# Pooled attention and a top-1 MoE on one core: V summed on two engines in the opening, another order of the first two units, K and V turned in full shapes, two weight pieces on GpSimd

## Chip, cores and metric

One core of a Trainium2 chip runs the whole program as one launch. The metric is device time in microseconds (us), median of three runs. Engines: PE (TensorE: matmuls and transposes), DVE (VectorE), ACT (ScalarE), POOL (GpSimd), SP (SyncE, which issues most transfers).

## The reference

```python
# q, k, v: (8 batches, 8 heads, 576 rows, 64), float32
k_p = k.reshape(B, H, 72, 8, D).mean(axis=3)        # 576 rows of K pooled to 72
v_p = v.reshape(B, H, 72, 8, D).mean(axis=3)
attn = softmax(scale * q @ k_p.T)                   # (.., 576, 72); 1e-9 is added to the sum
x = (attn @ v_p), heads side by side                # (4608 tokens, 512)
logits = x @ w_gate                                 # 8 experts
e, gate = argmax(logits), softmax(logits)[argmax]   # one expert for each token
y = gate * (relu(x @ w1[e]) @ w2[e])                # 512 -> 1024 -> 512
```

## The kernel before

**Attention** takes the span to about 182 us, **MoE** the rest. A *unit* is 128 query rows with all 8 heads: four units for each batch, and one more for the leftover rows of each pair of batches, 36 in all. Units go in groups of two. For a group `g_qt` (L477) turns q on PE, and ACT copies it to `qT`. `g_s` (L500) computes scores into one of two `ps` buffers, `g_min` (L510) takes the row maxima on DVE, `g_exp` (L517) is four exponentials on ACT. For a unit `u_pt` (L524, L526) turns P on PE and copies it on ACT, `u_pv` (L546) multiplies P by V into `po`, of which there is one buffer, and `u_nrm` (L573 to L575, DVE) divides by the row sums and so frees `po`. V is held in `VB` as [V | V times gate weights | 1], so `u_pv` yields the router's logits too.

**K and V of a batch** are loaded by SP into three buffers `kv[3]` (K of batch b in `kv[2b%3]`, V in `kv[(2b+1)%3]`). Their 576 rows lie in five chunks of 128 partitions, the last half full. The sum of 8 rows is made for b >= 2 on POOL in three steps (`pool`: L338 on 128x1280, L340 on 128x640, L341 on 128x320). `k_pe` turns K on PE (L379) into 64 partitions of PSUM, `k_act` copies that into half 0 of the block-diagonal `BD` (L391), and a transfer in ACT's queue (`moves`, L1037) copies half 0 to half 1. `v_pe` (L403, L405, and L407 for K's last 64 rows) turns V, `u_pe` (L424) multiplies it by the gate weights, and three operations on DVE lay the result into `VB`: `gates` (L431, reads PSUM), `masked_low` and `masked_high` (L436, two SBUF inputs: the sum of V and the mask `mk`).

**Order.** The code before L800 writes out the opening (batch 0: DVE sums K by `pool_now` and V by `pool_sum`, L360; the first scores; K of batch 1 summed on POOL from L812 and on DVE). Then one loop over the 36 units writes the code of each in a fixed order; `put(unit, position, f, args)` hangs more work at positions in it ("q" ahead of the unit, "pe", "act", "dve", "dve3", "sp"). Routing operations and the three that lay V are `fillers`, taken from a list a few at a time behind `u_pv`. `on_beat` makes a POOL operation wait for the last instruction in the list `beat`, which is the reciprocal (L574) of the unit before. `idle(n)` writes matmuls without use on PE, wide (512 columns) or narrow (128). `lsplit` (L868) makes the low part of the first expert's weights on DVE, in four pieces for each of eight j, pieces j=0 and 1 in units 13 to 16 and 18 to 21.

**MoE** is a loop over blocks of 256 tokens of one expert. Its tail takes the two halves of the finished block and scatters their rows: `give(1)`, then `give(0)` (L1278 on POOL), whatever the number of tokens.

## Time and profile before

| quantity | value |
|---|---|
| three runs | 595.24, 592.2, 591.74 us; median 592.2 |
| profiled execution, its own time | 594.74 us (span of the profile 592.1) |
| PE busy | 567.0 us, 96% of the span |
| DVE, ACT, POOL busy | 306.5, 276.4, 241.4 us |
| read from and written to memory | 73.65 and 23.37 MB |

The span is the time from the first to the last instruction of the profiled execution; the difference to its own time is what lies around it. PE is busy nearly everywhere, so what counts is PE's work itself, the places where PE stands idle, and the clock that it is granted (PEclk, 1.00 is 2.4 GHz). A row of stretches gives, for each engine, busy us and (x) the number of instructions. A row of the timeline is: start us, us, engine, line, operation, out<-in, xcount, and in brackets the idle time ahead of it and what ended it.

### The profile page before, as it was taken

Reading aid. Unit: us, or ns where it says so; the run is one execution under the profiler, and the core shown is the slowest. Engines: PE = TensorE matmul, PEld = TensorE weight load, DVE = VectorE, ACT = ScalarE, POOL = GpSimd, SP = SyncE. Lnnn points to the kernel's source line nnn. Section 1 sums busy time; section 2 is a strip of 40 time slices with the busy share of each in tenths; the row PEclk is TensorE's granted clock in tenths of the full one; section 3 lists DMA queues with packets and bytes.
Section 4 is the critical chain, followed back from the end, with each engine's and each line's share of the span. In section 5 each row is a group of like instructions: output and inputs, shape, how many; then the busy total and the mean of one; then the engine's idle time right before and its main releaser. Section 6 shows DMA issues by size and latency. Waiting matters only on the chain. (4 is left out here: it accounts for less than half of the span.)

```text
span 592.1 us, 15018 instructions
## 1 busy us (share of the span) xinstructions
PE 567.0 (96%) x4332; PEld 423.3 (71%) x4333; DVE 306.5 (52%) x639; ACT 276.4 (47%) x627; POOL 241.4 (41%) x465
## 2 busy tenths in 40 slices
PE   7989999999999989999999999999999999999993
PEld 6778998889885755775676676765767657767571
DVE  5776779997798272128312221272313723182783
ACT  4666788878942362227222222261223622272771
POOL 6495889884545222122222012231122311224255
PEclk8998999999999999999999999999999999999998
DMA  9997999857357959952943214339143491319310
GB/s 278 299 313 196 327 336 344 255 173 277 98 187 230 287 154 360 347 123 65 335 134 91 53 58 111 90 66 351 58 111 84 95 352 38 105 35 333 75 45 12
DMA packets 94072, 107.76 MB, mean 182 GB/s; under 512 B 53894, under 2 KB 62086, under 8 KB 94040
## 3 DMA queue, kind: packets, MB, share of 16 engines
q1 hardware_dynamic: 86408, 85.46, 49.6%
q0 software_dynamic: 6640, 20.99, 9.5%
q10 hardware_dynamic: 992, 0.92, 0.6%
q8 instruction: 16, 0.26, 0.2%
q14 instruction: 16, 0.13, 0.1%
HBM read 73.65 MB, written 23.37 MB: 164 GB/s over the span
## 5 line engine op out<-in xcount | busy, mean ns | idle before, releaser
L1067 PEld LDWEIGHTS <-bd 128*128 128x128 f16 x936 | 91.2, 98 | 105.7 <-DVE bd L1061 0.8
L1061 DVE SCALAR_TENSOR_TENSOR bd<-ps,bd 128x512 f16<-128x512 f32 (+1 forms) x44 | 27.5, 630 | 143.7 <-ACT bd L1057 143.2
L1277 POOL TENSOR_TENSOR spacer<-ql,iG 1x1 f32<-1x1 f32 x44 | 18.5, 420 | 166.2 <-ACT ql L1273 154.1
L517 ACT ACTIVATE both<-ps,nmx 128x72 f32<-128x72 f32 x288 | 70.0, 350 | 12.6 <-DVE nmx L510 12.2
L1067 PE MATMUL po<-w,bd 128*128 128x512 f16 x264 | 59.1, 379 | 0.0
L1067 PE MATMUL po<-kv,bd 128*128 128x512 f16 x264 | 58.8, 379 | 0.0
L546 PE MATMUL po<-vb,pt 128*128 128x146 f32 (+1 forms) x320 | 52.7, 311 | 5.5 <-DVE both L575 4.6
L1278 POOL DMA_INDIRECT out_dram<-ql,iG x44 | 47.1, 1071 | 22.0 <-issue 20.6
L1057 ACT ACTIVATE bd<-ps 128x512 f16<-128x512 f32 (+1 forms) x44 | 23.8, 547 | 69.2 <-PE L987 56.4
L546 PEld LDWEIGHTS po<-vb,pt 128*128 128x128 f32 x320 | 46.5, 192 | 8.4 <-issue 5.2
L1067 PE MATMUL pq<-kv,bd 128*128 128x512 f16 x216 | 48.1, 379 | 0.0
L989 PE MATMUL ps<-kv,qt 128*128 128x256 f16 (+1 forms) x176 | 44.8, 263 | 0.9 <-DVE qt L115 0.9
L677 POOL DMA_INDIRECT x_by_expert<-both,rpos x36 | 35.8, 996 | 23.2 <-issue 6.2
L987 PE MATMUL ps<-kv,w 128*128 128x256 f16 (+1 forms) x176 | 43.1, 258 | 2.3 <-DVE bd L906 1.8
L500 PE MATMUL ps<-bd,qT 128*128 128x144 f32 x256 | 45.0, 301 | 0.0
L987 PE MATMUL ps<-kv,qt 128*128 128x256 f16 (+1 forms) x176 | 44.8, 263 | 0.0
L988 PE MATMUL ps<-kv,qt 128*128 128x256 f16 (+1 forms) x176 | 44.8, 263 | 0.0
L989 PE MATMUL ps<-kv,w 128*128 128x256 f16 (+1 forms) x176 | 43.1, 258 | 0.0
L988 PE MATMUL ps<-kv,w 128*128 128x256 f16 (+1 forms) x176 | 43.1, 258 | 0.0
L1067 PE MATMUL pq<-w,bd 128*128 128x512 f16 x192 | 42.7, 379 | 0.0
L338 POOL TENSOR_TENSOR st<-kv 128x1280 f32<-128x1280 f32 x13 | 37.7, 2901 | 12.0 <-DVE ri L574 7.0
L1273 ACT ACTIVATE ql<-po,gB 128x512 f32<-128x512 f32 x22 | 15.1, 685 | 55.5 <-PE L987 41.6
(246 smaller groups left out, 1274.4 us busy)
## 6 DMA issues: line engine op xcount, KB each, us to landing
st<-in_moe_w_dram SPq DMA_DIRECT2D x8, 2048.0 KB, 13.8
both<-in_moe_w_dram SPq DMA_DIRECT2D x6, 2048.0 KB, 12.9
vb<-x_by_expert SPq DMA_DIRECT2D x16, 578.0 KB
kv<-in_v_dram SPq DMA_DIRECT2D x16, 512.0 KB
kv<-in_k_dram SPq DMA_DIRECT2D x7, 1024.0 KB
qt<-in_q_dram SPq DMA_DIRECT2D x7, 1024.0 KB
st<-in_moe_w_dram SPq DMA_DIRECT2D x4, 1024.0 KB
kv<-in_v_dram SPq DMA_DIRECT2D x8, 208.0 KB
```

The source lines that it names most:

```text
L338: on_beat(nc.gpsimd.tensor_tensor(t1, src[:, :, 0:4 * D], src[:, :, 4 * D:], op=OP.add))
L500: nc.tensor.matmul(ps[:, x * 2 * KP:(x + 1) * 2 * KP], t[:, h, :], BD[b % 3][:, :, h, :], start=True, stop=True)
L517: nc.scalar.activation(p[:, h * KP:(h + 1) * KP], ps[:, x * KP:(x + 1) * KP], AF.Exp, bias=nmx[:, x:x + 1], scale=-1.0)
L546: nc.tensor.matmul(po[:, cols], a[:, c * 128:(c + 1) * 128], VB[b % 3][:, c, sl, 0:CW], start=h in (0, LEFT), stop=False, skip_group_check ...
L677: st = nc.gpsimd.indirect_dma_start(out=xs, out_offset=bass.IndirectOffsetOnAxis(ap=Z["pos"][:, u:u + 1], axis=0), in_=X[:, u, :], in_offs ...
L987: nc.tensor.matmul(dst, wh, xT[:, d, 0:n], start=(d == 0), stop=False)
L988: nc.tensor.matmul(dst, wh, xT[:, DC + d, 0:n], start=False, stop=False)
L989: nc.tensor.matmul(dst, wl, xT[:, d, 0:n], start=False, stop=(d == DC - 1))
L1057: nc.scalar.activation(h, p, AF.Relu)
L1061: V.scalar_tensor_tensor(l, p, 0.0, h, op0=OP.max, op1=OP.subtract)
L1067: nc.tensor.matmul(y, hT[x][:, f, 128 * j:128 * j + 128], W2[s][z][:, f, :], start=(half == x == z == f == 0), stop=(half == z == 1 and f ...
L1278: st = nc.gpsimd.indirect_dma_start(out=out, out_offset=bass.IndirectOffsetOnAxis(ap=iG[:, j:j + 1], axis=0), in_=ys[j], in_offset=None, b ...
```

## The change

- **Opening.** V of batch 0: DVE sums three chunks, POOL two (`pool_pool`). V's chunks are laid in another order (`VK`, `HS`, `SLOTS`: the short one first). The warming matmuls go from 54 ahead of everything to 46 there, 22 narrow ones behind the turn of the gate weights and 4 more; that turn stands ahead of the second half of K, with three copies on ACT for five. The idle matmuls go from 5 wide to 11 wide.
- **Units 0 and 1** are written out by hand (`if i == 0`, `if i == 1`); `u_pt(1)` comes ahead of the turn of K of batch 1. That K is laid out doubled (`k1`, with three copies by `same` on DVE), so that it is turned by four full transposes and one small one, where it was four transposes, four matmuls and two small ones.
- **K and V of later batches** stand in one tile of ten 64-wide columns (`kvp`) and are turned as pairs, 128 columns at once: two transposes for K and three for V. K leaves PSUM in two copies, and its transfer becomes two.
- **Laying V:** `masked_low`, `masked_high`, `gates`, in that order; for batch 1 the two enter `beat`. The first step of V's sum of batch 2 on POOL moves to position "dve3" of unit 3.
- **Weights:** j=0 and 1 (eight operations of DVE) become `gsplit`, four 128x1024 operations of POOL in units 24, 25, 27 and 28.
- **Tail of the MoE loop:** `give(1)`, `give(0)` only where the block has more than one half filled, else the other way round.

```diff
-WARM = 54
+WARM = (46, 22, 4)
-VK = (0, 128, 216, 344, 472)
+VK = (472, 0, 128, 216, 344)
...
     def k_pe(b):
-        for c in range(4):
-            nc.tensor.transpose(pm[0:64, c * 128:(c + 1) * 128], kp[:, c], ident)
...
+        if b > 1:
+            for x in range(2):
+                nc.tensor.transpose(pm[:, 128 * x:128 * x + 128], pair(kp, 2 * x), ident)
+        else:
+            for x, o in enumerate((0, 1, 3, 4)):
+                nc.tensor.transpose(pm[:, 128 * x:128 * x + 128], pair(k1, o), ident)
...
     def k_act(b):
...
+            for s in range(2):
+                nc.scalar.activation(other(b, s, s), pm[64 * s:64 * s + 64, 0:256].rearrange("p (a x) -> p a x", a=2),
+                                     AF.Copy, scale=-SC)
+                moves.append((other(b, 1 - s, s), other(b, s, s), b))
...
     def v_pe(b):
...
+        for x in range(3):
+            nc.tensor.transpose(pm[:, x * 128:x * 128 + 128], pair(kvp, 4 + 2 * x), ident)
...
+            if b == 1:
+                beat.append(done)
...
-        fillers[0:0] = [(-1, False, f) for f in (gates, masked_low, masked_high)]
+        fillers[0:0] = [(-1, False, f) for f in (masked_low, masked_high, gates)]
...
+    def pool_pool(src, dst, c, out=None):
+        nc.gpsimd.tensor_tensor(t1[:, c], src[:, c, 0:4 * D], src[:, c, 4 * D:], op=OP.add)
+        nc.gpsimd.tensor_tensor(t2[:, c], t1[:, c, 0:2 * D], t1[:, c, 2 * D:], op=OP.add)
+        for o, i in out or ((c, c),):
+            nc.gpsimd.tensor_tensor(dst[:, o], t2[:, i, 0:D], t2[:, i, D:], op=OP.add)
...
-    pool_sum(kv[1], vp, slice(0, 1))
+    pool_sum(kv[1], vp, slice(1, 2))
+    pool_pool(kv[1], vp, slice(3, 5))
+    idle(5)
...
-    for c in range(2, 5):
-        pool_sum(kv[1], vp, slice(c, c + 1))
+    pool_sum(kv[1], vp, slice(2, 3))
+    pool_sum(kv[1], vp, slice(0, 1))
...
-                        put(POOLAT[b] + x + y, "q", f, b, y)
+                        put(*((3, "dve3") if (b, x, y) == (2, 2, 0) else (POOLAT[b] + x + y + (b == 2 and x == 2), "q")),
+                            f, b, y)
...
+    def gsplit(j, part):
+        src, t = st1[0][:, j], scratch[j]
+        if part == 0:
+            on_beat(nc.gpsimd.tensor_tensor(t, src, swc[:, 0:1].to_broadcast([128, F]), op=OP.mult))
+        else:
+            on_beat(nc.gpsimd.tensor_tensor(W1[0][1][:, j], t, W1[0][0][:, j], op=OP.subtract))
+
+    for at, j, x in ((24, 0, 0), (25, 0, 1), (27, 1, 0), (28, 1, 1)):
+        put(at, "q", gsplit, j, x)
...
+        if i == 0:
+            run(i, "q")
+            u_pv(0)
+            g_s(*A)
+            g_exp(*Y)
+            g_min(*A)
+            g_exp(*A)
+            u_pt(1)
+            run(i, "sp")
+            g_s(*Z)
+            u_nrm(i, lambda: g_min(*Z))
+            pool_k1(1)
...
+            g_qt(*turns[0])
+            continue
...
-        give(1)
...
-        give(0)
+        either(many > 1, lambda: [give(j) for j in (1, 0)], lambda: [give(j) for j in (0, 1)])
```

The next two pieces are DVE's instructions around the laying of V of batch 1 (`vb_161` before, `vb_162` after), ahead of unit 4's norm; the first is of before, the second of the change.

```order
L575 TENSOR_TENSOR both<-po,ri 128x576
L510 TENSOR_REDUCE nmx<-ps 128x4 x2
L431 TENSOR_TENSOR vb_161<-pq,mk 128x15x8
L436 TENSOR_TENSOR vb_161<-vp,mk 128x3x2x64
L436 TENSOR_TENSOR vb_161<-vp,mk 128x6x64
L573 TENSOR_SCALAR ri<-po 128x8
```

```order
L585 TENSOR_TENSOR both<-po,ri 128x576
L520 TENSOR_REDUCE nmx<-ps 128x4 x2
L444 TENSOR_TENSOR vb_162<-kvp,mk 128x3x2x64
L444 TENSOR_TENSOR vb_162<-kvp,mk 128x2x3x64
L438 TENSOR_TENSOR vb_162<-pq,mk 128x15x8
L583 TENSOR_SCALAR ri<-po 128x8
```

The two operations with two SBUF inputs (L436, now L444) have moved ahead of the one that waits for PE (L431, now L438); nothing else is between the two norms.

Next PE around the turn of K of batch 1 (L379 to L386 before, L391 and L393 after): `bd_157` and `bd_158` are the block-diagonal K of batches 0 and 1 before, `bd_159` that of batch 1 after; L524 and L534 turn P of unit 1.

```order
L500 MATMUL ps<-bd_157,qT 128x144 x2
L477 MATMUL pq<-ident,qt_154 128x128 x4
L379 MATMUL pq<-ident,kp 64x128 x4
L382 MATMUL pq<-ident,kp 64x128 x4
L385 MATMUL pq<-ident,kp 64x64
L386 MATMUL pq<-ident,kp 64x64
L500 MATMUL ps<-bd_157,qT 128x144 x2
L524 MATMUL pp<-ident,both 128x128 x5
L500 MATMUL ps<-bd_158,qT 128x144 x2
```

```order
L534 MATMUL pp<-ident,both 128x128 x5
L510 MATMUL ps<-bd_158,qT 128x144 x2
L487 MATMUL pq<-ident,qt_155 128x128 x4
L556 MATMUL po<-vb_161,pt 128x146 x3
L556 MATMUL po<-vb_161,pt 128x219
L556 MATMUL po<-vb_161,pt 128x146
L391 MATMUL pq<-ident,st_64 128x128 x4
L393 MATMUL pq<-ident,st_64 128x64
L487 MATMUL pq<-ident,qt_155 128x128 x4
L510 MATMUL ps<-bd_159,qT 128x144 x4
```

The turn of P of unit 1 (L534) and its P·V (L556) have moved ahead of the turn of K, which is half as many instructions; behind it only one turn of q stands ahead of the first scores that need it.

Last POOL in units 24 to 28, where the pieces of the first weights have come in between the scatters of tokens (L687): L911 multiplies, L913 subtracts.

```order
L911 TENSOR_TENSOR kv_152<-st_64,swc 128x1024
L686 MEMSET spacer 1x1
L687 DMA x_by_expert<-both,rpos 38016x578
L913 TENSOR_TENSOR w_01_61<-kv_152,w_00_60 128x1024
L686 MEMSET spacer 1x1
L687 DMA x_by_expert<-both,rpos 38016x578
```

Between them stood only the scatters before; the pair comes a second time for the other piece.

## Rows read from the trace of the kernel before

**Rows 1.** Stretches: window, length, busy us of PE, PEld, DVE, ACT, POOL; clock; DMA.

```profile
10.30:17.80 7.50, 7.50 (x36) 6.55 (x37) 4.65 (x8) 5.01 (x21) 0.00 (x0) 0.54 1.08 303
17.80:42.10 24.30, 22.98 (x173) 20.60 (x171) 17.36 (x29) 17.90 (x59) 18.32 (x11) 1.00 1.08 300
42.10:44.60 2.50, 0.02 (x1) 0.00 (x1) 2.43 (x5) 0.00 (x0) 2.42 (x3) 1.00 1.04 354
44.60:48.40 3.80, 3.77 (x16) 3.74 (x17) 2.12 (x7) 2.29 (x9) 2.68 (x2) 0.55 1.07 261
48.40:88.00 39.60, 38.42 (x320) 35.36 (x320) 27.87 (x81) 30.05 (x106) 30.96 (x28) 1.00 0.94 287
88.00:126.00 38.00, 35.31 (x301) 33.22 (x298) 35.43 (x93) 29.86 (x101) 33.08 (x31) 1.00 0.90 286
126.00:182.00 56.00, 55.33 (x486) 50.28 (x484) 46.30 (x169) 40.63 (x127) 30.96 (x55) 1.00 0.54 185
182.00:592.00 410.00, 397.39 (x2952) 268.05 (x2950) 164.02 (x228) 147.86 (x203) 114.00 (x296) 0.99 0.50 149
```

**Rows 2.** Timeline of the opening: the sum of V, the first P·V.

```profile
17.26 2.93 DVE L360 TENSOR_REDUCE vp<-kv 128x64 f32<-128x512 f32 x3
18.28 1.82 POOL L812 TENSOR_TENSOR st<-kv 128x768 f32<-128x768 f32 x1 [8.09 <-DMA kv<-in_k_dram]
...
20.11 1.89 DVE L436 TENSOR_TENSOR vb<-vp,mk 128x256 f32<-128x256 f32 x3
...
23.16 1.53 PE L546 MATMUL po<-vb,pt 128*128 128x146 f32 x10
...
27.39 2.90 POOL L338 TENSOR_TENSOR st<-kv 128x1280 f32<-128x1280 f32 x1 [4.94 <-DMA kv<-in_v_dram]
...
27.53 1.20 ACT L391 ACTIVATE bd<-pq 64x512 f32<-64x512 f32 x2 [0.35 <-PE pq L382]
```

**Rows 3.** Timeline at 38 us: POOL's sum beside DVE's laying of V.

```profile
38.25 2.90 POOL L338 TENSOR_TENSOR st<-kv 128x1280 f32<-128x1280 f32 x1
...
38.39 3.18 DVE L436 TENSOR_TENSOR vb<-vp,mk 128x384 f32<-128x384 f32 x1
...
38.39 4.99 DVE L436 TENSOR_TENSOR vb<-vp,mk 128x384 f32<-128x384 f32 x2
...
41.22 1.74 POOL L340 TENSOR_TENSOR st<-st 128x640 f32<-128x640 f32 x1
...
44.63 0.67 PE L546 MATMUL po<-vb,pt 128*128 128x146 f32 x2 [2.51 <-DVE both L575]
```

**Rows 4.** Timeline of PE's weight loads: a batch's V turn, then its K turn.

```profile
49.90 0.25 PEld L403 LDWEIGHTS pq<-ident,vp 128*128 128x128 f32 x2
50.12 0.11 PEld L405 LDWEIGHTS pq<-ident,vp 128*64 128x64 f32 x1
50.42 0.11 PEld L407 LDWEIGHTS pq<-ident,kp 64*64 64x64 f32 x1 [0.20 <-issue]
50.60 0.55 PEld L546 LDWEIGHTS po<-vb,pt 128*128 128x128 f32 x4
...
39.43 0.45 PEld L379 LDWEIGHTS pq<-ident,kp 128*64 128x64 f32 x4
39.88 0.55 PEld L500 LDWEIGHTS ps<-bd,qT 128*128 128x128 f32 x4
```

**Rows 5.** Stretches of the weight pieces L868 alone: length, DVE busy (count).

```profile
86.00:123.00 37.00, 6.82 (x8) 1.00 0.94 297
123.00:182.00 59.00, 10.61 (x24) 1.00 0.54 184
```

**Rows 6.** Transfers in ACT's queue (L1037): ns min/median/max, first and last start.

```profile
L1037 ACTq DMA_DIRECT2D bd<-bd x12: 468/468/553, 46.1 to 139.9; - x12
```

**Rows 7.** Timeline of POOL at the end: the last two scatters.

```profile
584.58 1.00 POOL L1278 DMA_INDIRECT out_dram<-ql,iG  x1 [0.56 <-issue]
...
586.62 1.00 POOL L1278 DMA_INDIRECT out_dram<-ql,iG  x1 [0.56 <-issue]
```

More of the change, by code (lines that the diff above doesn't have):

```diff
@@ L370, in pool_v, with pair, other @@
-        pool(kv[(2 * b + 1) % 3], KVS["vp", b], (part,))
+        pool(kv[(2 * b + 1) % 3], KVS["kvp", b][:, 5:10], (part,))
+    def pair(x, o):
+        return x[:, o:o + 2, :].rearrange("p c d -> p (c d)")
     def half(b, s):
         return BD[b % 3][64 * s:64 * s + 64, s].rearrange("p h x -> p (h x)")
+    def other(b, s, c):
+        return half(b, s)[:, 0:512].rearrange("p (a c x) -> p a c x", a=2, c=2)[:, :, c]
     def k_pe(b):
-        kp = KVS["kp", b]
+        kp = KVS["kvp", b]
         pm = KVS["pk", b] = psA.tile([128, 512], F32, name="pq", bufs=2)
-        for c in range(4):
-            nc.tensor.transpose(pm[0:64, c * 128:(c + 1) * 128], kp[:, c], ident)
@@ L380, in k_pe @@
-        if b == 1:
-            for c in range(4):
-                nc.tensor.matmul(pm[64:128, c * 128:(c + 1) * 128], kp[:, c], ident, start=True, stop=True)
-            pm, kt, it = psA.tile([128, 512], F32, name="pq", bufs=2), kp[0:64, 4], ident[0:64, 0:64]
-            KVS["pt", b] = pm
-            nc.tensor.transpose(pm[0:64, 0:64], kt, it)
-            nc.tensor.matmul(pm[64:128, 0:64], kt, it, start=True, stop=True)
+        if b > 1:
[4 more added lines that the diff above has]
+                nc.tensor.transpose(pm[:, 128 * x:128 * x + 128], pair(k1, o), ident)
+            pt = KVS["pt", b] = psA.tile([128, 512], F32, name="pq", bufs=2)
+            nc.tensor.transpose(pt[:, 0:64], pair(k1[0:64], 6), ident[0:64, 0:64])
@@ L399, in v_pe @@
+        nc.scalar.activation(half(b, 0)[:, 0:512], pm[0:64, :], AF.Copy, scale=-SC)
+        for c in range(2):
+            nc.scalar.activation(other(b, 1, 1 - c), pm[64:128, :].rearrange("p (a c x) -> p a c x", a=2, c=2)[:, :, c],
+                                 AF.Copy, scale=-SC)
+        pm = KVS.pop(("pt", b))
+        for s in range(2):
+            nc.scalar.activation(half(b, s)[:, 512:576], pm[64 * s:64 * s + 64, 0:64], AF.Copy, scale=-SC)
     def v_pe(b):
-        vp, kp = KVS["vp", b], KVS.pop(("kp", b), None)
+        kvp = KVS["kvp", b]
@@ L535, in u_pv @@
         PO_[i] = po[:, o0:o0 + H * CW]
-        for c in range(5):
+        for c in (1, 2, 3, 4, 0):
             sl = slice(*SLOTS[c])
@@ L733, in idle @@
                 nc.tensor.matmul(warm[:, 0, 0:128], ones, ones, start=True, stop=True)
-    vp = KVS["vp", 0] = work.tile([128, 5, D], F32, name="vp", bufs=2)
+    KVS["kvp", 0] = pooled(0)
+    nc.gpsimd.memset(KVS["kvp", 0][:, 4], 0.0)
+    vp = KVS["kvp", 0][:, 5:10]
     kp = st1[1].rearrange("p c x -> p (c x)")[:, 160:800].rearrange("p (c a d) -> p c a d", c=5, a=2)
-    KVS["kp", 1] = work.tile([128, 5, D], F32, name="kp", bufs=2)
-    idle(WARM, False)
+    KVS["kvp", 1] = pooled(1)
+    nc.gpsimd.memset(KVS["kvp", 1][:, 4], 0.0)
+    idle(WARM[0], False)
     constants()
@@ L767 @@
     k_keep(1, 0, 256)
+    turn_gates()
+    idle(WARM[1], False)
     pool_now(kv[0], kp, Z)
+    load_kv(1, vf)
     g_qt(0, 0)
+    idle(WARM[2], False)
     k_first((2, 3, 4))
-    k_keep(1, 256, 576)
     g_s(0, 0)
     k_keep(0, 256, 576)
+    k_keep(1, 256, 576)
     g_min(0, 0)
@@ L784 @@
     g_exp(0, 2)
-    pool_sum(kv[1], vp, slice(1, 2))
-    idle(2)
     g_s(0, 3)
@@ L789 @@
     g_exp(0, 3)
-    for c in range(2, 5):
-        pool_sum(kv[1], vp, slice(c, c + 1))
+    pool_sum(kv[1], vp, slice(2, 3))
+    pool_sum(kv[1], vp, slice(0, 1))
     gates, masked = u_dve(0)
+    load_kv(2, kf)
+    load_ql(0)
     g_qt(1, 0)
-    idle(2)
+    idle(4)
     u_pt(0)
+    g_s(1, 0)
     v_pe(0)
@@ L834, in prep @@
         put(u[0], "dve", u_dve, b)
-    prep(1, (0, "2"), (2, "2"), (3, ""))
+    put(2, "pe2", v_pe, 1)
+    put(2, "act2", v_act, 1)
+    put(3, "pe", u_pe, 1)
+    put(3, "dve", u_dve, 1)
     put(1, "sp", load_kv, 3, kf)
@@ L1002 @@
         Y = halves.get(2 * i - 1)
+        if i == 0:
[10 more added lines that the diff above has]
+            pool_k1(1)
+            same(k1[:, 2], k1[:, 0])
+            same(k1[:, 5], k1[:, 3])
+            same(k1[0:64, 7], k1[0:64, 6])
+            load_kv(2, vf)
+            g_qt(*turns[0])
+            continue
+        if i == 1:
+            run(i, "q")
+            g_exp(*Y)
+            u_pv(1)
+            u_nrm(i)
+            k_pe(1)
+            k_act(1)
+            g_qt(*turns[1])
+            run(i, "sp")
+            g_s(*A)
+            g_min(*A)
+            g_exp(*A)
+            g_s(*Z)
+            g_min(*Z)
+            continue
         if i < 30 and aged:
```

103 lines of the change are left out of this document (46 added, 57 removed).

## The prediction, made before the changed kernel had run

> **What bounds the kernel now.** I read first the page's busy shares, then the table of stretches, then the timeline where that table shows PE idle. PE is busy 567.0 of 592.1 us, so a gain must come from PE's own work, from its idle time, or from stretches at the lower clock. The stretches sort this [rows 1]. The MoE stretch (182 to 592) is 397 of 410 us PE at clock 0.99: the change touches only its tail. In the attention PE is idle 1.3 us in 17.8–42.1, 2.5 us in one piece at 42.1–44.6, 1.2 in 48.4–88, 2.7 in 88–126 and 0.7 in 126–182. The granted clock is 0.54 in 10.3–17.8 and 0.55 in 44.6–48.4, near the lower of the two levels; the second of these begins directly behind the idle 2.5 us.
>
> In the opening the first P·V starts at 23.16, at the end of a DVE chain: three V sums of 0.98 us from 17.26, then the laying of V from 20.11 [rows 2]. At 38 us there is another chain. POOL's first step of V's sum for batch 2 starts at 38.25 and takes 2.90. DVE's laying of batch 1 (two SBUF inputs) starts at 38.39 and shows 3.18 us, ending at 41.57, hardly after POOL has ended at 41.15. The second laying of the pair (together 4.99) runs beside POOL's next step, 41.22 to 42.96 [rows 3]. The norm that frees `po` queues behind both on DVE, and the P·V that waits for it comes at 44.63, after 2.51 us that ended with DVE's L575 [rows 3].
>
> The same collision is seen more weakly on the weight pieces: 8 pieces cost DVE 6.82 us at 86–123, where POOL sums batches, and 24 pieces 10.61 us at 123–182, 0.85 against 0.44 each [rows 5].
>
> **The change part by part.**
>
> *A, opening.* Two V sums leave DVE: 2 x 0.98 = 2.0 us earlier for the first P·V, if POOL has its two chunks ready in time; five chunks took 2.90 for the first step [rows 2], so two are far cheaper. Of this I take back 0.9: PE now reaches batch 1's turn of K with only one turn of q ahead of the scores that need it (the second pair of fences), and ACT's two copies of that K took 1.20 [rows 2]; they are now three. The copies were hidden by two turns and older scores before. The fillers and the earlier turn of the gate weights may keep the clock up in 10.3–17.8; at full clock that stretch's work would be 7.50 x 0.46 = 3.4 us shorter. I count none of it, since DVE's chain and not PE sets 23.16, but it is the upper bound's reason. On the other side DVE's laying of batch 0 could block with POOL's sum of K, which is about 1.82 in its first step [rows 2]. A: **+1.1**, bounds -1 to +2.2.
>
> *B, the stall at 42.* Now the two layings stand ahead of `gates`, thus do not wait for PE, and POOL's first step of batch 2 is ordered behind them by `beat` (first pair of fences). Alone they cost about the 1.89 that three such took in the opening [rows 2]. What goes: 2.5 us idle, and the low clock behind it, 3.8 x 0.45 = 1.7 [rows 1]. POOL's sum of V of batch 2 gets some 2 to 4 us later; it is needed only when batch 2 is turned, near 49.9 [rows 4]. Its first two steps ended at 42.96 [rows 3] and the third is half as large as the second, so over 5 us were to spare and the lateness hides. B: **+4.2**, bounds 2 (idle time returns in part, in smaller pieces that leave the clock alone) to 4.2.
>
> *C, turns in full shapes.* A batch's V turn spans 49.90 to 50.60, 0.70 with the gap of 0.20 ahead of the 64x64 one, and its K turn 39.43 to 39.88, 0.45 [rows 4]: 1.15. Now it is five instructions of 0.125: 0.62. Gain 0.53 for each of six batches (b=2 to 7), 3.2, and an estimated 0.1 each for `u_pe`, which waits for one copy of V instead of two: 3.8 in all. PE is 97–99% busy in 48.4–88 and 126–182 [rows 1], so most of it counts; in 88–126 DVE ends the waits and PE's work is hidden. I take about two thirds: **+2.6**, bounds 0 to 3.8.
>
> *D, eight weight pieces off DVE.* They take 6.82 us of DVE in 86–123 [rows 5], where DVE is busy 35.4 of 38 and PE is idle 2.7 [rows 1]. At most the 2.7 goes. Part of it is POOL against the routing operations, which stays. **+1.2**, bounds 0 to 2.7.
>
> *E, four GpSimd operations and six more transfers.* A 128x1024 operation lies between 1.82 (768) and 2.90 (1280): about 2.35 us [rows 2]. POOL has room, 31.0 busy of 56 in 126–182 [rows 1]. DVE's remaining pieces (j=2 and 3, units 22–25 and 27–30) meet them; by rows 5 a piece that meets POOL's work is 0.4 us longer, some eight pieces, 3.3 us on a DVE that has 10 of 56 free: **-0.5**, bounds 0 to -2.5. The K transfers in ACT's queue go from 12 to 18 at 0.47 [rows 6]: 2.8 us of ACT, which has 15 of 56 free and 8 of 38 in 88–126 [rows 1]; **-0.3**.
>
> *F, tail.* The last two scatters start 2.04 us apart [rows 7]. The last block is a half one (PE's matmuls there are 128 wide), so `give(0)` carries the rows and now goes first; the empty half's follows. What is gained is at most 2.0, if the empty scatter's end is not what the program waits for; I take a quarter: **+0.5**.
>
> **Sum:** 1.1 + 4.2 + 2.6 + 1.2 - 0.5 - 0.3 + 0.5 = 8.8. The profiled execution took 594.74, so 585.9 there; the median of the runs shown is 592.2, 2.5 below it, so **583.4**.
>
> **A rule that speaks against E.** The Trainium skill, page "SBUF — State Buffer", section "Who interferes with whom", says that a VectorE instruction with two SBUF inputs contends with a GpSimd instruction that reads SBUF, and that the one that starts first holds the shared port for the whole instruction while the other fully blocks. By that rule, at 38.39 the trace agrees: the second starter ended 0.42 us after the first [rows 3]. It speaks against putting `gsplit` beside DVE's weight pieces, which is the third rival below.
>
> **Rivals.**
>
> *Steady state gives nothing.* C and D are hidden behind DVE and ACT: what PE does not spend on turns it spends waiting for exponentials or norms. For it: in 88–126 PE's waits end with DVE, and ACT gets longer by the transfers. Against it: 98.8% PE busy in 126–182, where most of C falls [rows 1]. Then A + B + F - 0.8 = 5.0: 587.2.
>
> *The stall stays in another place.* POOL's K sum of batch 2 (an operation of 2.90 and one of 1.6 or so) now follows V's sums of batch 1 and might reach past 36.5, when the layings can start; then DVE's layings wait for that instead. B is worth nothing: 8.8 - 4.2 = 4.6, 587.6. Against it: POOL's V sum of batch 1 began at 27.39 [rows 2], done about 33, and the K sum's two longer steps would be over by about 38, so at worst the wait is for the second step, 1.74.
>
> *GpSimd's pieces hold DVE* (the other side). In units 24, 25, 27 and 28 a 2.35 us operation holds a laying or a weight piece of DVE, the norm is late behind it, PE stands, and the clock drops as at 42: 2.35 + 1.7 = 4.05 each, 16.2 in all. Gain without E's 0.5: 9.3, so 592.2 - 9.3 + 16.2 = 599.1. It decides the sign from an average loss of 2.3 us for each operation (9.3 / 4); slower by over 1% from 3.8. Against it: `on_beat` lets POOL start only behind a reciprocal, when DVE next does work from PSUM; and the collisions of rows 5 left the clock at 1.00.
>
> **How the numbers follow.** Forecast 0.64, steady state gives nothing 0.19, stall stays 0.11, GpSimd holds DVE 0.06. The likeliest's own range is 580 to 587: the distances to the bounds of A, B, C, D and E, added by squares, are about 3.5 on the side of a smaller gain and 3 on the other. With the two rivals of smaller gain (587.2 and 587.6, each uncertain by 1) the range is **579.0 to 588.5**; it leaves out the third rival, 0.06, and some 0.13 of tails (at 579 A's unpriced 3.4 of clock would have come in). A measurement of this kernel can tell about 1%, 5.9 us: faster means under 586.3, slower over 598.1. Faster: 0.60 of the forecast's 0.64, and 0.10 from the first two rivals' better ends: 0.70. Slower: the third rival, 0.06. Within 1%: 0.24.
>
> **What would show it.** In the changed profile: no idle piece of PE near 42 and clock 1.00 there (B); laying of batch 1 below 1.5 us each, POOL's first step starting behind it; first P·V near 21 (A); V and K turns of some 0.62 of weight loads for each batch, and PE's idle time in 48–182 not above 4.6 us (C, D); eight weight pieces fewer on DVE before 123 us; the four GpSimd operations near 2.35 us with DVE's pieces beside them near 0.85 and no idle PE over 1 us (E); the last scatter with rows about 2 us ahead of the other (F). I am wrong if a new idle piece of over 2 us or a stretch near clock 0.5 stands anywhere between 20 and 182, above all where `gsplit` runs, or if ACT's copies of batch 1's K stop PE for more than the 0.9 counted.

## The result: a little slower, and the profile after

The changed kernel takes 597.65 us (median of 10 runs, 594.95 to 599.37), the kernel before 592.55 in the same group of runs (10 runs, 591.52 to 595.24): ratio 1.007, interval 1.0047 to 1.0093. The forecast was 583.4 us. The profiled execution has a span of 595.8 us, [rows 1] came from one of 592.1.

The stretches of the changed kernel, with the columns of [rows 1]; the stretch that was 44.6–48.4 there is cut otherwise here, since the idle piece has moved:

```profile
10.30:17.80 7.50, 7.06 (x48) 5.14 (x47) 6.11 (x11) 5.59 (x20) 2.91 (x4) 1.00 1.07 321
17.80:42.10 24.30, 21.48 (x166) 19.95 (x166) 16.57 (x37) 18.47 (x63) 18.52 (x13) 1.00 1.09 301
42.10:46.80 4.70, 4.28 (x38) 3.45 (x38) 4.47 (x5) 3.68 (x13) 4.62 (x3) 1.00 1.07 300
46.80:50.00 3.20, 1.50 (x12) 1.29 (x11) 3.06 (x8) 0.80 (x2) 2.68 (x3) 1.00 1.10 193
50.00:56.00 6.00, 5.50 (x27) 5.21 (x27) 3.83 (x7) 2.94 (x11) 2.27 (x2) 0.50 1.15 236
88.00:126.00 38.00, 34.47 (x290) 32.43 (x290) 30.90 (x84) 30.21 (x102) 33.68 (x32) 1.00 0.89 281
126.00:182.00 56.00, 53.52 (x471) 49.00 (x470) 46.94 (x166) 39.94 (x124) 37.71 (x58) 1.00 0.55 184
182.00:592.00 410.00, 397.44 (x2952) 267.98 (x2949) 163.74 (x228) 147.73 (x203) 114.69 (x296) 0.99 0.49 149
```

The low clock of 10.3–17.8 and the idle piece at 42.1 are gone. In their place PE is idle 1.7 of 3.2 us from 46.8, and then comes a clock of 0.50 for six microseconds, which is the lower of the two levels. PE has more idle time in 88–126 (3.5 us, before 2.7) and in 126–182 (2.5, before 0.7).

Where each kernel stands against the other is best seen from the start of each unit's norm on DVE (L573 before, L583 after). Microseconds; in brackets the difference to before:

| unit | before | after |
|---|---|---|
| 0 | 26.01 | 22.43 (-3.6) |
| 1 | 31.65 | 25.82 (-5.8) |
| 2 | 35.18 | 32.99 (-2.2) |
| 4 | 47.53 | 41.07 (-6.5) |
| 5 | 52.27 | 48.32 (-4.0) |
| 7 | 61.37 | 59.52 (-1.9) |
| 30 | 156.58 | 155.54 (-1.0) |
| 33 | 168.04 | 168.01 (0.0) |

So the changed kernel was 6.5 us ahead at unit 4, more than the forecast of 5.3 for A and B together. It had lost all of it by the end of the attention, and lost 3.7 us more in the span after that.

**The tail.** POOL's timeline of the changed kernel at the end (L1350 writes the ids, L1352 scatters, L1351 stands between them):

```profile
577.11 1.81 POOL L1352 DMA_INDIRECT out_dram<-ql,iG  x1 [0.16 <-issue]
580.69 1.20 POOL L1350 TENSOR_TENSOR iG<-iB,zi 128x2 int32<-128x2 int32 x1 [1.77 <-DMA out_dram<-ql,iG]
...
585.94 0.19 POOL L1350 TENSOR_TENSOR iG<-iB,zi 128x1 int32<-128x1 int32 x1 [0.82 <-issue]
...
586.96 1.00 POOL L1352 DMA_INDIRECT out_dram<-ql,iG  x1 [0.57 <-issue]
589.42 0.18 POOL L1350 TENSOR_TENSOR iG<-iB,zi 128x2 int32<-128x2 int32 x1 [1.47 <-DMA out_dram<-ql,iG]
...
590.42 1.00 POOL L1352 DMA_INDIRECT out_dram<-ql,iG  x1 [0.56 <-issue]
```

`give(1)` copies two columns of ids, `give(0)` one. In the new order `give(1)` overwrites the column from which the transfer of `give(0)` still reads, and waits for it: 1.77 us in the last block but one, 1.47 in the last. In [rows 7] the last scatter starts at 586.62, now at 590.42.

**46 to 50 us.** The timeline of the changed kernel, POOL, DVE, ACT's queue and PE:

```profile
40.27 0.73 ACTq L1111 DMA_DIRECT2D bd<-bd  x1
...
41.10 0.60 ACTq L1111 DMA_DIRECT2D bd<-bd  x1
...
42.90 2.89 POOL L339 TENSOR_TENSOR st<-kv 128x1280 f32<-128x1280 f32 x1
...
43.20 2.65 DVE L634 TENSOR_TENSOR ra<-L,rm 128x32 f32<-128x32 f32 x1
...
45.88 1.57 DVE L640 SCALAR_TENSOR_TENSOR req<-ra,down 128x32 f32<-128x32 f32 x1
...
48.32 0.15 DVE L583 TENSOR_SCALAR ri<-po 128x8 f32<-128x8 f32 x1
...
49.01 0.51 PE L510 MATMUL ps<-bd,qT 128*128 128x144 f32 x2 [1.07 <-DMA bd<-bd]
```

Two things hold there. Small routing operations with two SBUF inputs (L634, L640) wait for POOL's sum of batch 3. And the first scores of batch 2 (L510 at 49.01) wait for a transfer of K to the other half, of which there are now two, issued at 40.27 and 41.10.

### The profile page after: what moved, and what is told of

Read it like the earlier page. It is cut to its first block, busy times and chain, and to the rows that moved or that the text cites. A ratio compares the mean times of both kernels' runs of the same rounds, so it can differ in the third digit from the quotient of the medians.

```text
span 595.8 us, 15183 instructions
## 1 busy us (share of the span) xinstructions
PE 563.8 (95%) x4328; PEld 420.7 (71%) x4329; DVE 305.8 (51%) x632; ACT 276.8 (46%) x624; POOL 251.8 (42%) x477
## 4 chain that ended last, share of the span: by engine, by line
PE 71%; DVE 8%; DMA 7%; ACT 6%; issue 4%; PEld 1%; POOL 1%; SPq 1%; ACTq 1%; POOLq 0%; DVEq 0%; PEldq 0%
PE po L1141 15%; PE pq L1141 13%; PE ps L1028 5%; PE ps L1030 5%; PE ps L1029 5%; PE po L556 5%; PE ps L510 3%; PE pp L1030 2%; PE pq L1030 2%; PE pp L1029 2%; PE pq L1028 2%; PE pq L1029 2%; PE pp L1028 2%; ACT both L527 2%; DMA vb<-x_by_expert 2%
## 5 line engine op out<-in xcount | busy, mean ns | idle before, releaser
L1351 POOL TENSOR_TENSOR spacer<-ql,iG 1x1 f32<-1x1 f32 x44 | 19.0, 432 | 169.8 <-ACT ql L1347 168.6
L556 PE MATMUL po<-vb,pt 128*128 128x146 f32 (+1 forms) x320 | 52.5, 311 | 7.4 <-ACT pt L536 4.5
L1352 POOL DMA_INDIRECT out_dram<-ql,iG x44 | 46.2, 1050 | 22.3 <-issue 20.9
L556 PEld LDWEIGHTS po<-vb,pt 128*128 128x128 f32 x320 | 46.7, 193 | 10.6 <-ACT pt L536 7.1
L510 PE MATMUL ps<-bd,qT 128*128 128x144 f32 x256 | 43.8, 294 | 2.7 <-DMA bd<-bd 1.1
L339 POOL TENSOR_TENSOR st<-kv 128x1280 f32<-128x1280 f32 x13 | 37.7, 2899 | 12.3 <-DVE ri L584 7.1
L687 POOL DMA_INDIRECT x_by_expert<-both,rpos x36 | 36.2, 1007 | 14.2 <-issue 5.9
L1347 ACT ACTIVATE ql<-po,gB 128x512 f32<-128x512 f32 x22 | 15.1, 685 | 58.2 <-PE L1029 42.1
```

The costliest lines, as they stand in the source:

```text
L339: on_beat(nc.gpsimd.tensor_tensor(t1, src[:, :, 0:4 * D], src[:, :, 4 * D:], op=OP.add))
L510: nc.tensor.matmul(ps[:, x * 2 * KP:(x + 1) * 2 * KP], t[:, h, :], BD[b % 3][:, :, h, :], start=True, stop=True)
L556: nc.tensor.matmul(po[:, cols], a[:, c * 128:(c + 1) * 128], VB[b % 3][:, c, sl, 0:CW], start=h in (0, LEFT), stop=False, skip_group_check ...
L687: st = nc.gpsimd.indirect_dma_start(out=xs, out_offset=bass.IndirectOffsetOnAxis(ap=Z["pos"][:, u:u + 1], axis=0), in_=X[:, u, :], in_offs ...
L1352: st = nc.gpsimd.indirect_dma_start(out=out, out_offset=bass.IndirectOffsetOnAxis(ap=iG[:, j:j + 1], axis=0), in_=ys[j], in_offset=None, b ...
```

## The experiments

Each is compared with the kernel before in its own group of runs. The chips differed: the kernel before took 593.0, 599.4, 597.1, 599.4 and 597.7 us in the five groups. So ratios are given. Two ratios of different groups can't be taken from one another, for only the kernel before ran in all five, and in some of the groups it seems to lose time that it doesn't lose in the first (the section on e6, e10 and e12 comes back to this). A profile is one execution: norms of unit 7 of one and the same attention code differ by up to 4.3 us between executions (the changed kernel, e1 and e2). A lead ("ahead") is always measured against the first profile of the kernel before.

### The tail undone (e1), the ids apart (e2), the tail alone (e3)

```diff
# e1_tail_back, against the changed kernel
-        many = entry(4, t, [ENG.Pool], 0, 3)
...
+        give(1)
...
-        either(many > 1, lambda: [give(j) for j in (1, 0)], lambda: [give(j) for j in (0, 1)])
+        give(0)
# e2_own_column, against the changed kernel
-        nc.gpsimd.tensor_tensor(iG[:, 0:j + 1], iB[:, 0:j + 1], zi.to_broadcast([128, j + 1]), op=OP.add)
+        nc.gpsimd.tensor_tensor(iG[:, j:j + 1], iB[:, j:j + 1], zi.to_broadcast([128, 1]), op=OP.add)
```

e3 is the kernel before with the changed tail and nothing else.

> The changed kernel with its tail as it was before: always give(1), then give(0), no count read by POOL. Theory (the tail's new order makes the second scatter's id write wait for the first scatter's transfer, 1.77 and 1.47 us in the trace of the changed kernel, and puts everything of the last block behind it): the 3.8 us by which the last scatter starts later are gone, 597.65 - 3.8 = 593.8. Rival (the loss lies in the attention or in the MoE loop, the tail only shows it): within 1 us of 597.6.

> The changed kernel with one edit in the tail: each give copies only its own column of ids, so that the second no longer writes a column that the first transfer may still read. Order and count stay as changed. Theory (the shared id column is the wait): 593.8, or up to 2 us less if the scatter with rows going first is worth something. Rival (the count that POOL reads and its branch cost the time): stays near 597.

> The kernel before with nothing but the changed tail. Theory (the tail alone costs 3.7 us): 592.55 + 3.7 = 596.3. Rival (the tail costs nothing in itself): 592.5.

Measured: e1 593.97 us, 1.0021 of before (0.9998 to 1.0044); e2 593.97, 1.0013 (0.9993 to 1.0032); e3 598.32, 1.0095 (1.0058 to 1.0132). POOL in e2 at the end:

```profile
581.59 1.00 POOL L1352 DMA_INDIRECT out_dram<-ql,iG  x1 [0.57 <-issue]
582.60 0.21 POOL L1350 TENSOR_TENSOR iG<-iB,zi 128x1 int32<-128x1 int32 x1
...
583.62 1.00 POOL L1352 DMA_INDIRECT out_dram<-ql,iG  x1 [0.56 <-issue]
```

The wait is gone and the two scatters are 2.03 us apart, as in [rows 7]. The tail is the cause of 0.5 to 0.9%, the shared column is the mechanism, and the count that POOL reads is innocent: e2 keeps it. The new order gains nothing even then. So the rest of the change, for which I forecast 8.3 us, was worth about nothing in this group (1.002).

### POOL's sum of batch 3 later (e4), shortened (e7), or no transfers of batch 2 (e8)

```diff
# e4_k3_late, on e1: units of POOL's sums of batch 3, and of its turns
+    LATE = ((6, "dve3"), (7, "q"), (8, "q"), (8, "q"))
...
-            if b == 1:
+            if b in (1, 2):
                 beat.append(done)
...
+                    prep(b, (8, ""), (10, ""), (11, ""))
# e7_short_k3, on e1
+        if (b, part) == (3, 0):
+            src = kv[(2 * b) % 3]
+            on_beat(nc.gpsimd.tensor_tensor(t1[:, :, 0:8], src[:, :, 0:8], src[:, :, 8:16], op=OP.add))
+            return
# e8_no_move_2, on e1
+            if m[2] != 2:
+                nc.scalar.dma_start(*m[:2])
```

> The changed kernel with the tail of before and, in the attention, POOL's sums of K and V of batch 3 two units later (their turns on PE later too, the laying of batch 2 ahead of them by a wait). Theory (the idle PE at 46 to 50 us and the low clock behind it come from routing operations with two SBUF inputs that meet the sum of K of batch 3): no L634 of 2.65 us, no idle stretch at 46 to 50, unit 7's norm some 5 us ahead of the kernel before instead of 1.85; if the lead lasts, 593.8 - 3 = 590.8. Rival (the stall comes from the transfer of K of batch 2, 1.07 us, or it returns at the next sum): unit 7 not over 2.5 us ahead, 593 to 594.5.

> The changed kernel with the tail of before, where the first step of POOL's sum of K of batch 3 works on 40 columns and not on 1280 (the sum of that batch's K is left out by this). Theory (the routing operations of units 0 to 3 with two SBUF inputs are held by that step): L634 at about 0.2 us, not 2.65; no idle PE of over 1 us at 46 to 50, clock 1.00 there; unit 7's norm 5 us or more ahead of the kernel before in the profile, 593.97 - 3 = 591. Rival (what holds there is the transfer of K of batch 2, issued at 45.9, landed at 49.0): a wait for that transfer of over 1 us stays, and the time is 593 to 594.5.

> The changed kernel with the tail of before, without the three transfers that copy K of batch 2 to the other half (half of that batch's scores is left out by this; the matmuls run as before). Theory of the transfer: the scores of batch 2 do not wait at 47 to 49, the low clock behind goes, 593.97 - 3 = 591. Rival, the collision of POOL and DVE: L634 and L640 still take 2.65 and 1.57, the norm of unit 5 is as late, 593.3 to 594.5.

Measured: e4 601.35, 1.0142 (1.0107 to 1.0176), a miss of the expectation: L634 took 0.18 us and unit 5 was 6.1 us ahead, so the collision went. But I had put batch 3's turn two units before its first scores, and those now waited for its transfers, 2.0 and 2.1 us; batch 2's waited 0.5 and 1.2. e7 and e8 change what the router sees, so the MoE has other blocks and the whole times (604.04 and 606.75) say nothing; only the attention is read. In e7's timeline the routing operation is short, yet the transfer still holds PE:

```profile
44.45 0.18 DVE L638 TENSOR_TENSOR ra<-L,rm 128x32 f32<-128x32 f32 x1
...
48.78 0.48 PE L514 MATMUL ps<-bd,qT 128*128 128x144 f32 x2 [1.19 <-DMA bd<-bd]
```

Its clock in 52–56 was 0.64 and unit 7 only 2.2 us ahead. In e8, without the transfers, the clock stayed at 1.00 and unit 7 was 5.2 us ahead, unit 30 still 4.4. Both theories are half right: with either thing taken away PE still stands idle there (in e8 2.4 us of 48–52). That the transfer is what drops the clock isn't shown by e8 alone, since e2, which has both things, also kept 1.00. Over all profiles it is likely: ten have two transfers for batch 2 and no useless matmuls, and the clock of 50–56 is 0.50 to 0.72 in nine of them and 1.00 in e2; in those of the changed attention with one transfer or none (e8, e15, e16, e17) it is 1.00.

### The transfers on SP (e5: all, e9: batches 3 to 7, e14: in the kernel before)

```diff
# e9_late_moves_sp, on e1 (e5: all on nc.sync; e14: this edit in the kernel before)
-            nc.scalar.dma_start(*moves.pop(0)[:2])
+            m = moves.pop(0)
+            (nc.sync if m[2] > 2 else nc.scalar).dma_start(*m[:2])
```

> The changed kernel with the tail of before, and the transfers that copy a batch's K to the other half of its block-diagonal issued by SP and not by ACT. Theory (the second transfer of a batch holds ACT another 0.5 to 0.7 us, ahead of the copy of P that P·V waits for: waits of 0.5 to 1.1 us on ACT at 75.9, 97.1, 114.3 and 135.0 us, which the kernel before does not have): these waits go, between unit 7 and unit 30 the kernel gains 2 to 3 us on the kernel before where it lost 0.8, 593.97 - 2.5 = 591.5. Rival (the turns in full shapes are hidden behind other work in any case): within 0.7 us of 594.

> The changed kernel with the tail of before, and the transfers of K of batches 3 to 7 issued by SP; those of batch 2 stay on ACT, because with them on SP a score waited 5.9 us for one. The tail of before alone stood at 1.002 of the kernel before. Theory (ACT's second transfer per batch is what turned the gain of the full-shape turns into a loss): no wait of P.V on ACT's copy of P of over 0.7 us between 65 and 140, the lead over the kernel before grows by 0.4 or more from unit 7 to unit 30 where it shrank by 0.6 to 0.8; 0.995 to 0.999 of the kernel before. Rival (the waits only change their place): 1.000 to 1.003.

> The kernel before with the transfers of K of batches 3 to 7 issued by SP; there each batch has one for K's first 512 columns and one for the rest. Theory (the doubling is what cost in the changed kernel): small gain, 0.997 to 1.000 of the kernel before. Rival (any transfer issued on ACT costs this much, so taking them off helps either kernel the same): 0.992 to 0.995.

What made me try it are these rows of the changed kernel's timeline: two transfers in ACT's queue, then ACT's copy of P, then the P·V that waited for it.

```profile
73.68 1.44 ACTq L1111 DMA_DIRECT2D bd<-bd  x2
...
75.16 0.70 ACT L536 ACTIVATE pt<-pp 128x640 f32<-128x640 f32 x1 [1.11 <-PE pq L487]
...
75.92 1.39 PE L556 MATMUL po<-vb,pt 128*128 128x146 f32 x8 [0.95 <-ACT pt L536]
```

Measured: e5 0.9991 (0.9968 to 1.0013), with this row of its waits (total, times, longest): a transfer of batch 2, which on SP stands behind loads.

```profile
PE ps L510 <- DMA bd<-bd: 5.9, 1, 5.9
```

e9 593.79 us, 0.9941 (0.9918 to 0.9964). As a ratio this is 0.8% under e1, in microseconds it is the same (593.97): the kernel before took 4.1 us more in this group, so the two ratios don't show what the transfers are worth. The profiles do, in part. The waits of P·V on ACT's copy of P (total, times, longest), of e1, of e9, and of e15 (below: one large transfer for each batch, on ACT):

```profile
PE po L556 <- ACT pt L536: 4.4, 7, 1.1
```

```profile
PE po L556 <- ACT pt L536: 1.4, 3, 0.7
```

```profile
PE po L554 <- ACT pt L534: 1.5, 4, 0.7
```

All seven profiles with two transfers a batch on ACT (the changed kernel, e1, e2, e4, e6, e7, e8) have seven or eight such waits, 3.9 to 4.8 us in all; no other has over 1.6. In e9 the lead grew from 3.0 us at unit 7 to 4.1 at unit 30, where in e1 it shrank by 0.8. So two transfers a batch on ACT cost some 2 to 3 us of PE's time in the attention, and either mending, SP or one transfer, takes that away. e14 is 1.0002 (0.9971 to 1.0033): in the kernel before, with one large transfer for each batch, taking it off ACT brings nothing that can be seen. That the doubling alone cost is not shown, though: e16 differs from e15, in one group, only by its single transfers on SP, and took 0.3% less, with intervals that overlap.

### K's turn as before (e15 with transfers on ACT, e16 with late ones on SP)

```diff
# e15_narrow_k, on e1 (e16: with the edit of e9 too)
-            for x in range(2):
-                nc.tensor.transpose(pm[:, 128 * x:128 * x + 128], pair(kp, 2 * x), ident)
+            for c in range(4):
+                nc.tensor.transpose(pm[0:64, c * 128:(c + 1) * 128], kp[:, c], ident)
...
+            nc.scalar.activation(half(b, 0)[:, 0:512], pm[0:64, :], AF.Copy, scale=-SC)
+            moves.append((half(b, 1)[:, 0:512], half(b, 0)[:, 0:512], b))
```

> The changed kernel with the tail of before and K of batches 2 to 7 turned as before: four transposes into 64 partitions, one copy, one transfer on ACT; V's turn stays in full shapes. The changed kernel with the tail of before stood at 1.002. Theory (the second transfer of K costs more than the two transposes save, some 0.2 us per batch): 0.996 to 0.999. Rival (the transfers are innocent): 1.001 to 1.004.

> As the kernel with K turned as before, and its single transfers of batches 3 to 7 on SP. Against the kernel with full-shape turns and late transfers on SP (0.994) it tells what the full shapes of K are worth once no transfer is on ACT. Theory (0.2 us of PE for each of six batches, hidden in part): equal to that kernel or up to 1.2 us slower, 0.994 to 0.996. Rival (the full shapes cost by their two copies and small packets): faster than it, under 0.993.

Measured: e15 594.92, 0.9929 (0.99 to 0.9957), more than expected; e16 592.35, 0.9895 (0.9863 to 0.9926). Set against e1 and e9 these ratios are 0.9% and 0.5% lower, but those ran in other groups, and e15 and e1 differ in microseconds the other way. In the group of e15 and e16 the kernel nearest to e9 is e13 (below; e9 with useless matmuls): 593.94 us, 1.6 more than e16, with intervals that overlap. So e16's number is on the side of its rival (the full shapes of K cost by themselves); no gain from them shows, and what they cost isn't clear of noise. One reason why they can cost shows in e15's timeline at batch 2, the single transfer and the first scores behind it:

```profile
40.62 0.56 ACTq L1109 DMA_DIRECT2D bd<-bd  x1
...
47.59 0.73 PE L508 MATMUL ps<-bd,qT 128*128 128x144 f32 x4 [0.75 <-DMA bd<-bd]
```

A transfer issued at 40.62 is awaited until 47.59. In e9 the two were issued at 40.92 and 41.74, and the scores wait twice:

```profile
47.99 0.48 PE L510 MATMUL ps<-bd,qT 128*128 128x144 f32 x2 [1.03 <-DMA bd<-bd]
49.75 0.51 PE L510 MATMUL ps<-bd,qT 128*128 128x144 f32 x2 [1.28 <-DMA bd<-bd]
```

The second half of K is there 1.8 us after the first. But one transfer can hold PE as well, when PE comes early enough. e3 has the attention of before; its profile shows the stall at 42 and then a wait for batch 2's single transfer, which the first profile of before doesn't have; behind it, in 52–56, the clock is 0.57:

```profile
42.85 1.61 PE L546 MATMUL po<-vb,pt 128*128 128x146 f32 x10 [1.93 <-DVE both L575]
...
52.27 1.01 PE L500 MATMUL ps<-bd,qT 128*128 128x144 f32 x4 [2.12 <-DMA bd<-bd]
```

The queue of these transfers on the two pages (packets, MB, share), of the changed kernel:

```profile
q10 hardware_dynamic: 2240, 0.92, 0.7%
```

and of the kernel before:

```profile
q10 hardware_dynamic: 992, 0.92, 0.6%
```

The same bytes go in more than twice the packets. What the later second half costs and what the smaller packets cost, no run tells apart.

### Useless matmuls in the idle time (e13, e17)

```diff
# e13_spin, on e9; e17_best, on e16
+                if (G, j) == SPIN:          # the first scores of batch 2
+                    spin(4 + x)             # 512 columns each, into a pq tile
                 nc.tensor.matmul(ps[:, x * 2 * KP:(x + 1) * 2 * KP], t[:, h, :],
```

> The kernel with late transfers on SP (0.994 of the kernel before), with nine wide matmuls without use ahead of and between the first two scores of batch 2, where PE stands idle for 1.0 and 1.3 us at 47 to 50 us. Theory (what eats the opening's lead is not only that idle time but the half clock that follows it, 50 to 56 us): the clock stays at 1.00 there in the profile, unit 7's norm is 5 us ahead of the first profile of before and not 3, and the time falls by another 1 to 2 us: 0.990 to 0.993. Rival (the idle time is the cost, or the useless matmuls delay the scores as much as the clock gave): 0.993 to 0.996, no change.

> The kernel with K turned as before and late transfers on SP (0.9895 of the kernel before), with the nine useless matmuls at the first scores of batch 2. Theory (the clock at 48 to 56 us falls in some executions only, and in the profile of that kernel it had not fallen, so the matmuls only guard against it): 0.987 to 0.990. Rival (they delay the scores, as one transfer now lands earlier): 0.990 to 0.993.

Measured: e13 0.9918 (0.9892 to 0.9944), e17 0.9893 (0.9867 to 0.9918). The stretches of e13,

```profile
46.80:50.00 3.20, 2.52 (x14) 1.34 (x13) 1.68 (x6) 1.18 (x5) 3.12 (x3) 1.00 1.21 184
50.00:56.00 6.00, 5.83 (x52) 5.59 (x50) 4.88 (x15) 3.89 (x13) 3.24 (x3) 1.00 1.13 277
```

and of e9, which lacks only the matmuls:

```profile
46.80:50.00 3.20, 0.89 (x6) 0.55 (x5) 2.73 (x6) 1.03 (x3) 3.12 (x3) 1.00 1.16 213
50.00:56.00 6.00, 5.94 (x40) 5.72 (x40) 3.82 (x8) 2.84 (x11) 2.63 (x2) 0.72 1.14 282
```

With PE occupied the clock stayed at 1.00, PE did 52 instructions in 50–56 and not 40, and unit 7 was 4.8 us ahead, not 3.0. This is one execution, and e2 kept the clock without such matmuls. In time the step from 0.9941 to 0.9918 lies within the intervals, and the groups differ; a gain in time is not shown. On e16 the matmuls change nothing (0.9893 against 0.9895): there the clock had stayed up without them. e16 and e17 are the fastest of all, 1.05% under the kernel before in their groups.

### One part alone: laying V (e11); weight pieces back on DVE (e6, e10, e12)

e11 is the kernel before with the new order of laying and POOL's step behind it (`beat`, position "dve3"). e6 is e1, e10 is e9, with these lines, and e12 is e10 with the tail of e2:

```diff
+    for j, at in ((0, (13, 14, 15, 16)), (1, (18, 19, 20, 21)), (2, (22, 23, 24, 25)), (3, (27, 28, 29, 30)),
...
-    for at, j, x in ((24, 0, 0), (25, 0, 1), (27, 1, 0), (28, 1, 1)):
-        put(at, "q", gsplit, j, x)
```

> The kernel before with one part of the change: V of a batch laid in the order masked, masked, gates; for batch 1 POOL's first step of the next sum ordered behind it. My forecast of that part: 4.2 us less, 0.993 of the kernel before. Rival (the lead is given back at 46 to 56 us, where batch 2's first scores wait for POOL's sums and a transfer, or routing operations meet POOL, and the clock falls there instead): 0.998 to 1.002, with a stretch of low clock between 46 and 60 in the profile.

> The changed kernel with the tail of before and all weight pieces on DVE as before, none on GpSimd. Theory (GpSimd's four operations delay the scatters of tokens and so the first block's load and its transposes by 4 us, on which PE waits at unit 33): the lead over the kernel before is not lost by 1 to 1.4 us between units 30 and 33; against that, DVE's eight pieces come back at units 13 to 21, and cost up to 1.2 by my forecast. So 593.97 - 1.2 + (0 to 1.2): 592.8 to 594. Rival (DVE's pieces do cost what I forecast and the scatters have slack): 595.

> As the kernel with the late transfers on SP, and the eight weight pieces on DVE as before. Theory (GpSimd's four operations delay the scatters and the first block's load): no wait of the first block's matmuls at unit 33, 1.0 to 1.5 us under the kernel with the transfers alone: 0.993 to 0.997 of the kernel before. Rival (the pieces on DVE cost at units 13 to 21 what they save at unit 33): as the kernel with the transfers alone.

> The changed kernel with three mendings: each half's scatter copies its own column of ids (order as changed), late transfers on SP, eight weight pieces on DVE. It differs from the kernel with the transfers and the pieces only in the tail. Theory (with the shared column gone the order is worth nothing, as the scatters' ends do not depend on it): equal to that kernel within 0.2%. Rival (rows first is worth up to 2 us once nothing waits): 0.3% less than that kernel.

Measured: e11 1.0004 (0.9982 to 1.0027). In its stretches the idle piece at 42 and the low clock behind it are gone, as I had said,

```profile
40.00:44.00 4.00, 4.00 (x33) 3.90 (x33) 2.87 (x8) 2.80 (x10) 2.99 (x2) 1.00 1.04 358
44.00:48.00 4.00, 4.00 (x35) 3.47 (x34) 2.42 (x8) 3.42 (x13) 3.92 (x3) 1.00 0.97 308
```

and the time is that of before: from -1.6 us at unit 7 it came to +1.3 at unit 30. The rival's outcome is right; its low clock between 46 and 60 did not show in this profile, the lead was lost at units 24 to 27. e6 0.9992 (0.997 to 1.0015), e10 0.998 (0.9959 to 1.0002), e12 0.9976 (0.9952 to 0.9999, equal to e10 as expected). e10 against e9, in one group, says that the pieces on DVE cost 0.4% (2.2 us, intervals that overlap by 0.05%), against my theory; e6 against e1 points the other way by 0.3%, from other chips and with the intervals overlapping. The profiles of e6, e10, e11, e12 and e14 all lose 2 to 4 us at units 24 to 27 where e9 and the first profile of before lose none; what PE and DVE wait for there (both are put down to matmuls that had ended half a microsecond before) I could not settle.

The profiles do show which kernels have this loss, and where. The five that have it are the five from the groups at 597 to 599 us that keep the eight pieces on DVE: from unit 20 to unit 30 they lose 2.3 to 3.6 us. The eight from those groups with the pieces on GpSimd (e5, e7, e8, e9, e13, e15, e16, e17) change there by -0.7 to +0.5. Then, from unit 34 to 35, the five lose 1.2 to 1.3 and the eight 2.2 to 2.8. In the group at 593.0 neither happens: e3, with the pieces on DVE, loses nothing from unit 20 to 35. The kernel before has the pieces on DVE too; it was profiled in none of the slower groups, but probably loses as much there, and what moving the pieces is worth depends on the group: 0.4% in that of e9, nothing that shows between e6 and e1. The ratios of e9, e13, e15, e16 and e17 then contain this gain, and can't be held against e1's. e6 and e10 both have the pieces on DVE, as before has, and differ only in the late transfers: 0.9992 and 0.998, within the intervals.

## Why the prediction was wrong, point by point

- **A, opening (+1.1): right in mechanism, too small.** The first P·V came at 19.82, not 23.16 [rows 2]: 3.3 us earlier, forecast 2.0. The low clock of 10.3–17.8, on which I counted nothing, is gone. For batch 1's copies I took back 0.9; the turn of q that waits for them shows 1.20. The lead falls by 3.6 us between units 1 and 2 (-5.8 to -2.2), but that is not the price of the copies: K's turn now stands behind unit 1's P·V, where it stood ahead of it, so unit 1 alone gains by it. What A left at unit 2 is 2.2 us. From the timeline of the changed kernel:

```profile
19.82 1.64 PE L556 MATMUL po<-vb,pt 128*128 128x146 f32 x10 [0.33 <-DVE vb L438]
...
27.63 0.66 PE L487 MATMUL pq<-ident,qt 128*128 128x128 f32 x4 [1.20 <-ACT bd L405]
```

- **B, the stall at 42 (+4.2): the step fails as a gain.** The laying of batch 1 came ahead of POOL's sum of V, L444 at 35.29 in 2.10 us for both where L436 took 4.99 [rows 3], POOL's step behind it at 37.47. It still met the end of POOL's K sum (L341 to 35.84, L342 to 36.98); in e11, where POOL stood idle beside it, it took 1.02:

```profile
39.84 1.02 DVE L436 TENSOR_TENSOR vb<-vp,mk 128x384 f32<-128x384 f32 x2
```

  But the 4.2 us were not there to be had by this alone: e11 gains nothing. What I did not ask is what an earlier PE meets next. It met POOL's next sums with routing operations, and a transfer of K: 4.6 of the 6.5 us at unit 4 were gone at unit 7. Also, the idle piece and its low clock were read from one execution of 594.74 us, 2.5 above the median of the three; the sum took them as present in all. In e3 and e14, with the same code up to there, the wait was 1.93 and 1.04 us and the clock behind it stayed at 1.00, and then the first scores of batch 2 waited 2.12 and 1.86 for K's transfer. So 1.7 of the 4.2, the low clock, is not there in every execution of the kernel before, and the rest is in part what the transfer takes back.
- **C, full shapes (+2.6): the saving on PE is right, its price is not.** The weight loads of the two turns are 0.24 and 0.36, 0.60 in all, against the forecast 0.62 and 1.15 before [rows 4]. PE's weight loads of the changed kernel:

```profile
37.03 0.24 PEld L388 LDWEIGHTS pq<-ident,kvp 128*128 128x128 f32 x2
...
43.52 0.36 PEld L415 LDWEIGHTS pq<-ident,kvp 128*128 128x128 f32 x3
```

- **E, six more transfers (-0.3): the cost was in the waits, some ten times the term.** I multiplied six by 0.47 [rows 6] and set it against ACT's idle time. Their median is 0.60 now, two stand in a row ahead of ACT's copy of P, and the second half of K lands up to 1.8 us after the first (e9), where the first scores of a batch wait for it. P·V waits 4.4 us for ACT's copies in e1, 1.4 in e9 and 1.5 in e15: 3 us for a term of 0.3. From unit 7 to 30, where C should have brought most of its 2.6, the kernels with these transfers lose 0.6 to 0.8 us (the changed kernel, e1, e2), while e9 gains 1.1 and e15 0.8. What it comes to in the whole time, no two kernels of one group show.

  The row of the changed kernel that answers to [rows 6]:

```profile
L1111 ACTq DMA_DIRECT2D bd<-bd x18: 492/597/743, 40.3 to 139.1; - x18
```

- **D and GpSimd's pieces (+1.2 - 0.5): right in one group, not seen in another.** e9 is 2.2 us under e10 (one group); e6 against e1 shows no gain. The four operations took 1.90 and 2.12 us each, two of either, below my 2.35; the rival that they hold DVE and drop the clock did not come.
- **F, tail (+0.5): wrong sign, -3 to -5.** The bounds "0 to 2.0" left out a loss. [rows 7] shows the two scatters; that the writes of ids ahead of them are 128x2 and then 128x1 stood in the same timeline, and would have told that the other order makes the second write hit what the first transfer reads.
- **Sum.** A + B + C + D + E were 8.3 us, of which the group of e1 shows nothing (1.002). In the profile of the changed kernel the account is: 6.5 us ahead at unit 4 (forecast for A and B 5.3), 4.6 lost from there to unit 7, 0.8 to unit 30, 1.0 to unit 33, and 3.7 behind the attention. So two steps failed. The stall at 42 was booked as a gain without the next wait, at K's transfers, which E priced by their issue time; and the tail was given no bound on the side of a loss. With the tail and K's turn undone and late transfers on SP (e16) the time is 1.05% under before, 6.3 us, but in a group where e14, which is near to the kernel before, loses 3.2 us at units 20 to 30 with the pieces on DVE; how much of the forecast gain e16 would show in the first group is not known.
- **The rivals.** "The stall stays in another place" had the right idea and the wrong place: the laying behind POOL's K sum lost about 1.1 us (2.10 against 1.02), and what held PE were routing operations and a transfer, later. Of what I named as making me wrong, the clock near 0.5 between 20 and 182 and a wait of over 0.9 for ACT's copies (1.20) are in the profile; an idle piece of over 2 us is not. A chance of 0.70 for faster by over 1% was too high for a change of so many parts.

The Trainium skill, page "SBUF — State Buffer", section "Who interferes with whom", which I had weighed for GpSimd's weight pieces, applied elsewhere: L634 took 2.65 us beside L339 and ended with it, and in e7, without that, 0.18. The trace agrees. For the transfers, its page "DMA: Bandwidth & Descriptors", section "Issuing engines are not separate DMA queues", says that transfers of all issuing engines run on the same 16 DMA engines. The trace fits with this and does not prove it: 64 KB from SBUF to SBUF took 7.1 us (median) from issue to landing in e1 at 36–56 us, where all 16 engines are busy with loads (DMA share 1.05 to 1.15 in 40–50).
